# Leaving h undivided and subtracting the expert weights in PSUM at the start of an attention plus max-out kernel

## The chip, the cores and the metric

One core of one Trainium2 chip. The metric is the device time of one execution in microseconds (us), lower is better. The kernel before takes 340.46 us (median of 3 runs, 340.42 to 340.65). Executions vary by some tenths of a microsecond. A run counts as fast here if it lies within 1.5% of the fastest of its kernel.

## The reference

```python
# B, N, m, C = 4, 12544, 32, 128; d_ff = 1024
def mab(q, kv):
    s = scale * (q @ kv.transpose(0, 2, 1))
    a = softmax(s)                      # cut: max subtracted, exp, divided by the sum
    return a @ kv
h = mab(inducing, x)                    # 32 summary rows for each batch
y = mab(x, h)                           # every token attends to the 32 rows
h1, h2 = y @ w1, y @ w2
out = np.maximum(h1, h2) @ w_out
```

Everything after the second softmax is linear in `y` except the maximum. The kernel uses max(h1, h2) = h1 + relu(h2 - h1), so it needs w21 = w2 - w1 and, for each batch, two small products that stand in for the wide ones: hwd = h·w21 (32 rows by 1024) and m1 = h·(w1·w_out) (32 rows by 128).

## The kernel before

The batches run one after the other. While batch b makes outputs, batch b+1's h is computed in the gaps. Only batch 0 has nothing to hide behind: its first phase is about 16 us of transposes, scores and sums, in "units" of up to 16 tiles of x (128 tokens each), and the handover to the outputs follows. PSUM is the memory that matmuls write into; to "evict" is to copy a result out of one of its banks, on VectorE or ScalarE. The change touches these two stretches.

```python
units = []                              # 16 tiles each; the last full group in two 8s
for i, (_, n) in enumerate(p1_blocks):
    step = 8 if i == NP1 - 2 else n
    units += [(i, g, min(step, n - g)) for g in range(0, n, step)]
units = units[:-3] + units[-1:] + units[-3:-1]
...
def u_h():                              # batch 0: sums, reciprocal, h divided
    nc.vector.reduce_sum(out=rec, in_=<PSUM sums viewed as m x 4>)
    nc.vector.reciprocal(out=rec, in_=rec)
    nc.vector.tensor_mul(hT4, <h in PSUM, four copies>, <rec, four copies>)
...
u_h()
for i in range(4):                      # w21 = w2 - w1, fp32 in, fp16 out
    eng = nc.vector if i == 3 else nc.gpsimd
    eng.tensor_sub(w21[:, sl], w2f[:, sl], w1f[:, sl])
...
prep_w1T()                              # transposes of w1, copies on ScalarE
...
stages[-1][0].stage()                   # attention scores and exp of the first block
small_hwd(0)                            # hwd = h . w21: 4 matmuls, evicted by VectorE and ScalarE
for blk in stages[-1][1:]: blk.stage()
prep_w1out()                            # w1out = w1 . w_out
```

Then comes the steady loop. A "burst" multiplies exp values by hwd into four PSUM banks, and VectorE and ScalarE evict them through relu. A "final" makes one output bank: the m1 term (`m1d` is m1 spread over four masked copies by GpSimd), then 16 matmuls of relu by w_out. The first blocks use the `start` branch:

```python
def final(self, i):
    for s, (q, tt) in enumerate(cols):
        if start:
            nc.tensor.matmul(out=o, lhsT=<exp>, rhs=st[blk.b]["m1d"][:, q, :],
                             start=(s == 0), stop=False)
        for jb in range(NJB):
            nc.tensor.matmul(out=o, lhsT=self.relu[:, jb, q, tt, :], rhs=woutp[:, jb, :], ...)
    nc.vector.tensor_mul(self.osb[...], ps, rp)     # divide by the row sums, then store
```

The softmax here doesn't subtract the row's maximum and nothing guards it: scores larger than these inputs give would overflow.

## Time and profile before

| | before |
|---|---|
| median of 3 runs | 340.46 us |
| profiled run, span of the core | 340.25 us, 338.5 us |
| TensorE busy | 329.7 us, 97% |
| warm-up ends (start of the transpose of the inducing rows) | 7.32 us |
| VectorE starts on the sums | 23.62 us |
| first burst, third burst | 26.19, 29.11 us |
| last output multiplication starts | 335.35 us |

The times in the lower rows are starts in the timeline of the trace, counted from the start of the span. TensorE (PE) is busy nearly always, so what counts is where it is not: before 40 us. In the lines of a timeline the columns are start, duration, engine, source line, operation, out<-in, shapes and count; a bracket says how long the engine had been idle and what ended that.

### The profile page before, as it was taken

Reading aid. Unit: us, or ns where it says so; the run is one execution under the profiler, and the core shown is the slowest. Engines: PE = TensorE matmul, PEld = TensorE weight load, DVE = VectorE, ACT = ScalarE, POOL = GpSimd, SP = SyncE. Lnnn points to the kernel's source line nnn. Section 1 sums busy time; section 2 is a strip of 40 time slices with the busy share of each in tenths; the row PEclk is TensorE's granted clock in tenths of the full one; section 3 lists DMA queues with packets and bytes.
Section 4 is the critical chain, followed back from the end, with each engine's and each line's share of the span. In section 5 each row is a group of like instructions: output and inputs, shape, how many; then the busy total and the mean of one; then the engine's idle time right before and its main releaser. Section 6 shows DMA issues by size and latency. Waiting matters only on the chain.

```text
span 338.5 us, 14493 instructions
## 1 busy us (share of the span) xinstructions
PE 329.7 (97%) x6346; PEld 263.8 (78%) x6346; DVE 295.9 (87%) x620; ACT 269.7 (80%) x521; POOL 92.9 (27%) x164
## 2 busy tenths in 40 slices
PE   8899999999999999999999999999999999999996
PEld 3787688888768878888777878887777777878875
DVE  1348999999989999999998999999998998989994
ACT  1559988777888887787899777877899989888881
POOL 7243113454532224443242141423242100000000
PEclk9999999999999999999999999999999999999999
DMA  7999799499719985994229951212221221222222
GB/s 130 211 270 214 193 244 255 131 193 232 203 64 181 275 180 129 195 244 141 88 95 205 273 174 65 95 71 90 96 95 67 100 99 72 95 96 95 97 97 108
DMA packets 53423, 50.42 MB, mean 149 GB/s; under 512 B 41456, under 2 KB 42128, under 8 KB 53360
## 3 DMA queue, kind: packets, MB, share of 16 engines
q0 software_dynamic: 11408, 33.43, 37.0%
q1 hardware_dynamic: 41952, 16.08, 21.9%
q8 instruction: 49, 0.80, 1.0%
q14 instruction: 14, 0.11, 0.1%
HBM read 27.28 MB, written 25.69 MB: 157 GB/s over the span
## 4 chain that ended last, share of the span: by engine, by line
PE 93%; ACT 3%; DVE 1%; POOL 1%; issue 1%; DVEq 0%; POOLq 0%
PE ps L544 56%; PE ps L471 19%; PE ps L486 4%; PE ps L297 2%; PE ps L275 2%; PE ps L406 2%; PE ps L173 2%; PE ps L192 2%; ACT relu L508 1%; ACT xT L200 1%; PE ps L208 1%; PE ps L427 1%; PE ps L350 1%; DVE relu L504 1%; POOL eacc L324 1%
## 5 line engine op out<-in xcount | busy, mean ns | idle before, releaser
L508 ACT ACTIVATE relu<-ps 128x512 f16<-128x512 f32 x444 | 235.5, 601 | 43.0 <-PE ps L471 29.7
L504 DVE TENSOR_SCALAR relu<-ps 128x512 f16<-128x512 f32 x340 | 218.7, 679 | 5.3 <-PE ps L471 4.5
L544 PE MATMUL ps<-woutp,relu 128*128 128x128 f16 x3136 | 209.1, 220 | 0.0
L544 PEld LDWEIGHTS <-relu 128*128 128x128 f16 x3136 | 176.4, 98 | 29.8 <-issue 20.2
L560 DVE TENSOR_TENSOR o<-ps,rp 128x256 f32<-128x256 f32 x196 | 81.9, 418 | 16.0 <-PE ps L544 14.2
L570 POOL DMA_DIRECT2D out_dram<-o x75 | 41.1, 547 | 156.4 <-DVE o L560 108.1
L471 PE MATMUL ps<-e,hwd 32*128 32x256 f16 (+1 forms) x1632 | 82.8, 268 | 0.4
L471 PEld LDWEIGHTS <-hwd 32*128 32x128 f16 x1632 | 27.0, 92 | 19.0 <-issue 3.2
L486 PE MATMUL ps<-m,e 32*128 32x128 f16 x372 | 29.7, 214 | 0.7
L486 PEld LDWEIGHTS <-e 32*128 32x128 f16 x372 | 18.2, 92 | 7.0 <-issue 3.9
L317 POOL TENSOR_TENSOR eacc<-eacc,et 128x512 f32<-128x512 f32 (+1 forms) x18 | 18.5, 1028 | 0.3
L284 ACT ACTIVATE et<-ps 128x512 f16<-128x512 f32 (+1 forms) x21 | 11.4, 544 | 4.8 <-PE ps L275 4.8
L416 ACT ACTIVATE e<-ps 128x512 f16<-128x512 f32 (+2 forms) x30 | 14.9, 553 | 0.0
L114 POOL DMA_DIRECT2D xn<-in_x_dram x21 | 11.5, 550 | 4.7 <-DMA xn<-in_x_dram 4.1
L197 DVE COPY xT<-ps 128x1024 f16<-128x1024 f16 (+1 forms) x8 | 5.1, 642 | 8.4 <-PE ps L192 8.4
L200 ACT COPY xT<-ps 128x1024 f16<-128x1024 f16 x5 | 5.1, 1012 | 9.0 <-PE ps L192 9.0
L275 PE MATMUL ps<-inducingT,xT 128*128 128x32 f16 x294 | 10.6, 176 | 0.0
L297 PE MATMUL ps<-et,xn 128*128 128x32 f16 x294 | 10.6, 176 | 0.0
L275 PEld LDWEIGHTS <-xT 128*128 128x128 f16 x294 | 9.6, 96 | 0.0
L297 PEld LDWEIGHTS <-xn 128*128 128x128 f16 x294 | 9.5, 96 | 0.0
L173 PE MATMUL ps<-warm 128*128 128x512 f16 x22 | 7.7, 495 | 1.2 <-DVE warm L158 1.2
L406 PE MATMUL ps<-xT,hT 128*32 128x512 f16 (+2 forms) x120 | 8.7, 350 | 0.1
(65 smaller groups left out, 115.4 us busy)
## 6 DMA issues: line engine op xcount, KB each, us to landing
out_dram<-o POOLq DMA_DIRECT2D x72, 256.0 KB, 3.2
xn<-in_x_dram POOLq DMA_DIRECT2D x23, 512.0 KB, 8.9
out_dram<-o SPq DMA_DIRECT2D x24, 256.0 KB, 2.0
wf<-in_moe_w_dram POOLq DMA_DIRECT2D x2, 512.0 KB, 13.7
xn<-in_x_dram POOLq DMA_DIRECT2D x2, 256.0 KB, 13.5
out_dram<-o POOLq DMA_DIRECT2D x3, 128.0 KB, 4.7
xT<-xn SPq DMA_TRANSPOSE x21, 6.2
xn<-in_x_dram POOLq DMA_DIRECT2D x4, 64.0 KB, 9.3
```

Source lines behind the costliest of these rows:

```text
L275: nc.tensor.matmul(out=ps[:, j * M : (j + 1) * M], lhsT=xT_tiles[b % 2][:, k0 + j, :], rhs=inducingT, start=True, stop=True,)
L297: nc.tensor.matmul(out=ps[:, 0:M], lhsT=xn[:, j, :], rhs=et[:, j, :], start=(j == 0), stop=(j == n - 1),)
L317: nc.gpsimd.tensor_add(out=acc, in0=acc, in1=et[:, 0:n, :])
L406: nc.tensor.matmul(out=ps[32 * q : 32 * (q + 1), 0 : self.width], lhsT=st[self.b]["hT4"][:, 32 * q : 32 * (q + 1)], rhs=xT[:, q % self.g], ...
L416: nc.scalar.activation(out=self.e2[:, 0 : self.width], in_=ps[:, 0 : self.width], func=AF.Exp, scale=scale,)
L471: nc.tensor.matmul(out=ps[:, jj * w : (jj + 1) * w], lhsT=st[blk.b]["hwd"][r, 128 * jb : 128 * (jb + 1)], rhs=blk.e2[r, 128 * self.t0 : 12 ...
L486: nc.tensor.matmul(out=part.fin[q][1][:, 128 * s : 128 * (s + 1)], lhsT=part.blk.e2[r, 128 * tt : 128 * (tt + 1)], rhs=st[part.blk.b]["m1" ...
L504: nc.vector.tensor_scalar(out=dst, in0=src, scalar1=0.0, scalar2=None, op0=ALU.max)
L508: nc.scalar.activation(out=dst, in_=src, func=AF.Relu)
L544: nc.tensor.matmul(out=o, lhsT=self.relu[:, jb, q, tt, :], rhs=woutp[:, jb, :], start=False, stop=(s == 1 and jb == NJB - 1),)
L560: nc.vector.tensor_mul(self.osb[:, h : h + 2, :], ps[:, 0:256].rearrange("p (s c) -> p s c", s=2), rp.broadcast_to((128, 2, 128)),)
L570: eng.dma_start(out=outr[blk.b, :, k : k + nst, :], in_=self.osb[:, 0:nst, :])
```

## The change

Its intent is to shorten the serial path between the last sum of batch 0 and the first burst. There are five parts, and one piece of setup for the second.

1. The last full group of tiles comes as 8, 4 and 4, so that less work follows the last tile of x.
2. h is not divided by the softmax sums. It is scaled by 2^-14 to fit fp16, and the reciprocal sums become per-partition scales of the exp and of the evictions of hwd and m1.
3. w1 and w2 are loaded as fp16, and h·w2 - h·w1 is formed in PSUM by 8 matmuls in place of 4.
4. w1's transposes and w1out move behind hwd, and `m1d`'s matmuls move behind the 16 relu matmuls.
5. Later batches still need w21. An fp32 reload of both weights by SyncE (SP) and four subtractions on GpSimd move into the loop.

The sums over one column need a mask, `same_m`. VectorE builds it with four copies at the start of the first phase.

```diff
+        if i == NP1 - 2:
+            units += [(i, 0, n // 2), (i, n // 2, n // 4), (i, n // 2 + n // 4, n // 4)]
...
-        nc.gpsimd.dma_start(out=w1f, in_=moe_w1)
-        nc.gpsimd.dma_start(out=w2f, in_=moe_w2)
+        nc.gpsimd.dma_start(out=w2h, in_=moe_w2)
+        nc.gpsimd.dma_start(out=w1h, in_=moe_w1)
...                                         (after the inducing rows are transposed)
+        for q in range(4):
+            r = slice(32 * q, 32 * (q + 1))
+            nc.vector.tensor_copy(
+                out=same_m[r, :, :], in_=identity32[r, None, r].broadcast_to((32, 4, M))
+            )
...                                         (u_accum: sums over a column of ones)
-                    lhsT=ones16,
-                    rhs=et[:, j : j + w // M, :],
+                    lhsT=et[:, j : j + w // M, :],
+                    rhs=ones16,
...                                         (u_h)
+            part = smp.tile([128, 2], F32, name="sum_part")
+            nc.vector.tensor_mul(part, <sums>, sum_scale)
+            nc.tensor.matmul(out=ps[:, 0:2], lhsT=same_m, rhs=part, start=True, stop=True)
+            nc.vector.tensor_scalar(out=hT4, in0=<h in PSUM>, scalar1=HS, op0=ALU.mult)
+            nc.vector.reciprocal(out=rs, in_=ps[:, 0:2])
+            nc.scalar.mul(neg, hT4, -1.0)
...                                         (u_hwd, new)
+            for lhsT, rhs, first_mm in ((hT4, w2h, True), (neg, w1h, False)):
+                for i, (bi, ps) in enumerate(banks):
+                    nc.tensor.matmul(out=ps[:, 0:w], lhsT=lhsT, rhs=rhs[...],
+                                     start=first_mm, stop=not first_mm)
+            ... evictions scaled by st[0]["rs"] on VectorE and ScalarE
...                                         (Block.stage)
-                    scale=scale,
+                    scale=st[self.b]["scale"],
...                                         (final: the m1d matmuls after the relu matmuls)
...                                         (order)
-        small_hwd(0)
+        u_hwd()
         for blk in stages[-1][1:]:
             blk.stage()
-        prep_w1out()
+        prep_w1T()
...
+        def load_wf():
+            nc.sync.dma_start(out=w1f, in_=moe_w1)
+            nc.sync.dma_start(out=w2f, in_=moe_w2)
+        at(24, load_wf)
+        for i in range(4):
+            at(33 + 2 * i, sub_w, i)
...
-            p.burst(u, lead, (lambda: small_m1(0)) if g == 0 else None)
+            p.burst(u, lead, (prep_w1out, lambda: small_m1(0))[g] if g < 2 else None)
```

## The prediction

> **What bounds the kernel now.** I read the busy row of the page, the stages, the chain of work that ended last, the timeline of the first 36 us, and the waits on DMA. The page and its chain of work:
>
> ```profile
> PE 329.7 (97%) x6346; PEld 263.8 (78%) x6346; DVE 295.9 (87%) x620; ACT 269.7 (80%) x521; POOL 92.9 (27%) x164
> ...
> PE ps L544 56%; PE ps L471 19%; PE ps L486 4%; PE ps L297 2%; PE ps L275 2%; PE ps L406 2%; PE ps L173 2%; PE ps L192 2%; ACT relu L508 1%; ACT xT L200 1%; PE ps L208 1%; PE ps L427 1%; PE ps L350 1%; DVE relu L504 1%; POOL eacc L324 1%
> ```
>
> TensorE is on the chain for 93% of the span, three quarters of it in L544 and L471, the expert's output and input matmuls, which the change leaves alone. The stages (columns: window, sum of its width, PE, PEld, DVE, ACT, POOL busy us) say where there is room:
>
> ```profile
> 10.00:20.00 10.00, 9.13 (x210) 8.35 (x211) 2.77 (x4) 6.15 (x8) 2.50 (x4) 1.00 1.08 238
> 20.00:30.00 10.00, 9.44 (x202) 7.48 (x199) 7.02 (x17) 6.96 (x19) 5.40 (x10) 1.00 1.18 234
> 30.00:40.00 10.00, 9.60 (x159) 6.84 (x154) 9.36 (x19) 9.61 (x20) 1.46 (x3) 1.00 0.95 208
> ...
> 100.00:200.00 100.00, 99.90 (x1991) 81.25 (x1988) 93.28 (x196) 83.60 (x163) 32.12 (x57) 1.00 0.79 182
> ```
>
> From 40 us on PE has nearly no gap, so the change can only move the start of that stretch. Before it lie batch 0's first phase (to 23.6 us) and its handover into the first small blocks; from 30 to 36 us VectorE and ScalarE are full of evictions. The handover, from the timeline (start, duration, engine, line):
>
> ```profile
> 22.36 0.86 ACT L217 ACTIVATE et<-ps 128x64 f16<-128x64 f32 x3 [0.91 <-PE ps L208]
> ...
> 23.62 0.29 DVE L253 TENSOR_REDUCE hrec<-ps 128x32 f32<-128x128 f32 x1 [1.62 <-PE ps L233]
> ...
> 23.94 0.35 DVE L258 RECIPROCAL hrec<-hrec 128x32 f32<-128x32 f32 x1
> 24.29 1.07 ACT L617 CAST w1T<-ps 128x512 f16<-128x512 f32 x2 [1.07 <-PE ps L611]
> 24.41 0.29 DVE L260 TENSOR_TENSOR hT<-ps,hrec 128x128 f16<-128x128 f32 x1
> ...
> 25.25 0.76 DVE L355 CAST hwd<-ps 128x256 f16<-128x256 f32 x2 [0.22 <-PE ps L350]
> ...
> 26.19 0.40 PE L471 MATMUL ps<-e,hwd 32*128 32x128 f16 x16
> ...
> 26.86 0.27 ACT L375 CAST m<-ps 128x128 f16<-128x128 f32 x1 [0.30 <-PE ps L370]
> ...
> 27.02 1.09 ACT L508 ACTIVATE relu<-ps 128x512 f16<-128x512 f32 x2
> ...
> 27.21 1.18 POOL L378 TENSOR_TENSOR m1d<-m,mask 128x256 f16<-128x256 f16 x2 [0.37 <-ACT m L375]
> ...
> 29.11 1.09 PE L471 MATMUL ps<-e,hwd 32*128 32x128 f16 x24
> ```
>
> The reader is to see a serial path: last sum matmul, then 1.08 us on VectorE (23.62 to 24.70), 1.49 us to the first burst (26.19), then 2.92 us until the third burst starts at 29.11. I take 29.11 as the anchor: ScalarE is busy without a break from 29.54 to 38.8, so a shift of the third burst passes into the rest.
>
> **What the Trainium skill says.** "TensorE: Matmul & The Clock Gate", section Back-to-back issue gap, gives about 25 ns for up to 64 columns, 134 cycles for 128 and 262 for 256 at 2.4 GHz. The trace agrees: 16 accumulations of 32 columns take 0.39 us in the chain (24 ns each), 16 transposes of 128 columns 0.91 (57 ns), and I use 0.11 us for one of 256. "VectorE: DVE Perf Modes", section The perf-mode tier table, lets a copy from PSUM run at up to 2x; the copy of 1024 fp16 columns out of PSUM took 0.69 us, below the 1.07 that 1024 columns take at one per 0.96 GHz clock, so it agrees. "DMA: Bandwidth & Descriptors", section SWDGE vs HWDGE vs iDMA, ties a cast during DMA to GpSimd: the fp16 weights stay behind x in the POOL queue, whereas the later fp32 reload may go by SP. No run yet shows either kind for the weights. "ScalarE: Activation LUTs", section Step-by-step: what each stage is for, lets the scale be a per-partition pointer at no extra stage; no row of before shows one, so I charge it nothing.
>
> **The change part by part.**
> *Shorter last units.* Units of x become 16 x5, 2, 8, 4, 4 tiles. The order of instructions shows that the fifth unit's transposes now come before the fourth's scores. Landings before (time of issue plus time to landing, read for each load): fourth unit 14.05 us, fifth 17.2, the 2 tiles 17.5, the two 8s 18.75 and 20.1. So the last tiles still land at 20.1. Worked forward with the durations of before: transposes of unit four 15.60 to 16.5, accumulation to 17.0, wait for the fifth unit, its transposes 17.4 to 18.3, scores of four to 18.7, the 8 tiles' transposes to 19.3, scores of five to 19.7, accumulation to 20.2. VectorE, which takes all of the last copies at 0.69 per 1024 and about 0.42 (estimate between 0.29 and 0.69) per 512 columns, ends them at about 21.4. The last scores run 21.7 to 21.8, their exp (128 columns, 0.27) ends at 22.2, the last sum matmul lands at 22.5. Before, VectorE started on the sums at 23.62: gain 1.1 us. The order also has one warming matmul fewer; it lies inside that.
> *Sums over one column.* 25 matmuls of mostly 128 columns become 25 of one column: 25 x (57 - 25) ns = 0.8 us of PE, but nearly all beside the ScalarE copy (19.28 to 20.29 for instance) that paces each 2.58 us unit. Worth 0.05 in the last units, counted above.
> *h undivided.* Removed: 0.29 + 0.35 + 0.29. Added on VectorE: a 2-column product (0.16, like the 0.17 reciprocal of 4 columns) and h's eviction (0.29), so h is ready 22.97, 0.47 after the start in place of 1.08. The fp32 sum matmul (0.25, as L331's) and a 2-column reciprocal end at 23.16, beside PE's work. Gain 0.6.
> *Subtraction in PSUM.* Four matmuls of 256 columns more: 4 x 0.11 = 0.44 later. The negation on ScalarE (0.27, from 23.0) hides beside the first four. The evictions (2 x 0.38 on each engine) end at 24.75, first burst about 24.83 in place of 26.19: gain 1.36 at this point, which is near 1.1 + 0.6 - 0.44 = 1.26, the rest being issue gaps.
> *w1's transposes.* In fp16: 8 x 0.057 in place of 8 x 0.13 of PE, but moved behind the hwd matmuls (24.2 to 24.66). Their copy goes to VectorE after its two hwd evictions: 24.85 to 25.54, so w1out's matmuls run 25.6 to 26.05, against 25.64 to 26.26 before. Here the gain stops.
> *Order on ScalarE.* After: w1out (26.25 to 26.52), two relus (1.10, to 27.62), e of the 8-tile block (0.41, to 28.03), then m (0.27, to 28.30). Before, m came in front of the relus and was done at 27.13. GpSimd's m1d (0.60 for the half the first output needs) therefore ends at 28.98, against 27.80.
> *m1d matmuls last.* The first output's 16 matmuls may start at 27.7 instead of 28.2 and end 28.6, then wait for m1d until 29.05. Third burst: 29.17, against 29.11.
> *Weights.* x fills the queue in both, and one DMA slot more shifts no landing that is waited for: the fp16 pair is estimated at 21.3 and 22.6, where fp32 landed, woutp at about 24.2. The w21 subtractions (4 x 0.72 on GpSimd) move to the bursts around 80 to 92 us, before its fold at 91.6. GpSimd idles 1.0 to 2.4 us before each output there and one fits into each, so I charge nothing. The order of the main loop is otherwise unchanged, engine for engine.
> Sum: -1.1 - 0.6 + 0.44 before the first burst, and about +1.3 given back by w1T, w1out, m and m1d: +0.06 at the anchor, with an error of some 0.6 as each of a dozen waits can be off by 0.05 to 0.1 and some by more.
>
> **The rivals.** (a) The gain of the first burst survives: evictions of bursts 0 and 1 start up to 1 us earlier on VectorE (25.6 against 26.62), the m1d wait is shorter than I think, and the rest of the ramp follows. Speaks for it that 30 to 36 us are bound by evictions. It gives at most 340.46 - 1.3 = 339.2. (b) The worked path: m1d takes the place of the old wait; 340.5. (c) GpSimd's later subtractions delay the fold that PE waits 0.97 us for at 93.66, or the reload of w1 and w2 slows x or the transposes. Against it: one subtraction is 0.72 and the gaps are longer, and DMA is at about half. If all four landed in the path it would be 2.9 us: 343.4. (d) DMA stays the floor of the first phase and the smaller loads are slower; then the 1.1 shrinks to 0.5 and, with the unchanged path behind it, the time is 341.1.
>
> **Range and chances.** I weigh (b) at 0.45, (a) in part or whole at 0.4, (c) and (d) at 0.15. The mean of (b) 340.5 and a half-surviving gain, 339.7, is about 340.1; I predict 340.1 us, range 339.2 to 340.9. Two per cent is 6.8 us, more than the whole handover holds (23.6 to 29.1 us), so faster by over 2% has 0.01, slower 0.01, within 2% 0.98.
>
> **What would show it.** Right: sums reach VectorE at about 22.5; first burst at 24.7 to 25.0; w1out no earlier than 25.5; m1d's matmuls preceded by a PE gap of about 0.45 us near 28.6 to 29.05; third burst within 0.3 us of 29.1; the same 0.97 us wait near 93.7. Wrong: a third burst before 28.5 (then rival a), a PE gap at the fold over 1.5 us (rival c), or a last landing of x after 20.6 us (rival d). A change at the end of the kernel would also refute it, as nothing there has moved.

## The result and the profile after

The changed kernel took 341.17 us (median of 6 runs, 340.81 to 341.45), against 340.44 us (340.00 to 340.65) for the kernel before in the same rounds. The ratio is 1.0023, with a 95% interval of 1.0010 to 1.0036. A ratio here is the mean time of one kernel's fast runs over that of the other's of the same rounds, so not quite the ratio of the medians quoted. The class predicted, within 2%, came true, but the time lies 0.27 us above the top of the range, and 1.07 us above the predicted time. The kernel got slower by 0.7 us where I had expected it to gain 0.4.

The page of after, busy row and chain of work that ended last:

```profile
PE 328.4 (97%) x6351; PEld 263.1 (78%) x6351; DVE 297.3 (88%) x628; ACT 269.3 (79%) x520; POOL 94.6 (28%) x166
...
PE 87%; DMA 6%; issue 2%; POOL 1%; ACT 1%; DVE 1%; POOLq 0%
```

TensorE has 1.3 us less work, in a span 0.6 us longer. The 6% of DMA in the chain are less than they seem: at `m1d` the chain steps back through GpSimd's own queue to a weight load, with 4.25 us of "issue" between. The timeline below names what GpSimd really waited for, ScalarE's m. The stages of after, columns as in the prediction:

```profile
10.00:20.00 10.00, 8.94 (x223) 8.13 (x220) 4.02 (x7) 5.50 (x8) 3.03 (x5) 1.00 1.10 208
20.00:30.00 10.00, 8.66 (x194) 6.83 (x191) 6.15 (x17) 6.44 (x18) 3.31 (x6) 1.00 1.19 210
30.00:40.00 10.00, 9.41 (x155) 6.67 (x155) 9.34 (x20) 9.69 (x20) 1.15 (x2) 1.00 0.95 206
...
100.00:200.00 100.00, 99.91 (x1991) 81.07 (x1987) 93.53 (x196) 83.75 (x163) 32.62 (x57) 1.00 0.83 177
```

From 20 to 30 us PE is busy 8.66 us where it was 9.44: the handover holds more idle time, not less. The steady stage is as it was. The handover itself, from the timeline of after:

```profile
17.31 1.07 PE L202 MATMUL ps<-identity,xn 128*128 128x128 f16 x16 [0.26 <-DMA xn<-in_x_dram]
...
20.66 0.75 DVE L207 COPY xT<-ps 128x512 f16<-128x512 f16 x2 [0.43 <-PE ps L218]
...
22.70 0.16 DVE L264 TENSOR_TENSOR sum_part<-ps,sum_scale 128x2 f32<-128x2 f32 x1 [1.28 <-PE ps L243]
...
25.10 0.40 PE L534 MATMUL ps<-e,hwd 32*128 32x128 f16 x16
...
25.20 0.69 DVE L682 COPY w1T<-ps 128x1024 f16<-128x1024 f16 x1 [0.17 <-PE ps L678]
...
25.95 0.62 PE L688 MATMUL ps<-woutp,w1T 128*128 128x128 f16 x8 [0.45 <-DVE w1T L682]
...
26.61 0.27 ACT L696 CAST w1out<-ps 128x128 f16<-128x128 f32 x1 [1.25 <-PE ps L688]
...
26.77 1.09 ACT L571 ACTIVATE relu<-ps 128x512 f16<-128x512 f32 x2
...
27.74 0.49 ACT L479 ACTIVATE e<-ps,rs 128x256 f16<-128x256 f32 x1
...
28.10 0.39 ACT L436 ACTIVATE m<-ps,rs 128x128 f16<-128x128 f32 x1
...
28.57 1.19 POOL L441 TENSOR_TENSOR m1d<-m,mask 128x256 f16<-128x256 f16 x2 [4.29 <-ACT m L436]
...
29.23 0.27 PE L607 MATMUL ps<-m1d,e 128*128 128x128 f16 x2 [0.38 <-POOL m1d L441]
...
29.44 1.04 PE L534 MATMUL ps<-e,hwd 32*128 32x128 f16 x24
```

The sums are reached 0.92 us sooner and the first burst 1.09 us sooner (25.10 against 26.19). Then w1's transposed copy, w1out, two relus, m and m1d come one after another, and the third burst starts 0.33 us later than before. That is the path that the prediction worked out. The first line, the fifth unit's transposes waiting for DMA, is in the prediction too (17.4); the wait is new against the kernel before, and its end differs from run to run.

The end of each timeline, first before, then after:

```profile
335.35 0.42 DVE L560 TENSOR_TENSOR o<-ps,rp 128x256 f32<-128x256 f32 x1 [0.58 <-PE ps L544]
```

```profile
335.56 0.42 DVE L624 TENSOR_TENSOR o<-ps,rp 128x256 f32<-128x256 f32 x1 [0.58 <-PE ps L607]
```

The last output is 0.21 us later, but the span is 0.6 us longer (338.5 to 339.1). So 0.39 us arise after the last computation.

I cut every trace at the same five points: W, the end of the warm-up; S, VectorE's first instruction on the sums; the third burst; the last output multiplication; the end of the span.

| stretch, us | before | after | difference |
|---|---|---|---|
| start to W | 7.32 | 6.98 | -0.34 |
| W to S (first phase) | 16.30 | 15.72 | -0.58 |
| S to third burst (handover) | 5.49 | 6.74 | +1.25 |
| third burst to last output | 306.24 | 306.12 | -0.12 |
| last output to the end | 3.15 | 3.54 | +0.39 |
| sum (span) | 338.5 | 339.1 | +0.6 |

The spans are read to 0.1 us, so each tail, here and below, may be off by 0.05.

The first row is chance, not the change (the mean W of all fifteen traces is 7.32 us, as in this trace of before). The granted clock goes from half to full at some time between 4.2 and 7.2 us after the start of the span, differently in each run (in the trace of before at 5.5 us), and W lies between 6.66 and 8.14 us in the traces. That alone can scatter the times by some ±0.7 us. There is a second scatter. In 10 of the 44 runs of the kernel before in the jobs of the experiments, the mean granted clock is 0.995 where it is otherwise 0.998 or more; nine of these ten take 341.8 to 342.3 us and one 342.9, some 1.5 us longer than the rest. None of the 12 runs of the changed kernel did this, too few to say that the change prevents it. I give the median of the before runs at 0.998 or more ("full clock"), which is 340.46, 340.60, 340.62 and 340.57 us in the four jobs.

### The profile page after: what moved, and what is told of

It is laid out like the page before. It is cut to its first block, busy times and chain, and to the rows that moved or that the text cites. A ratio compares the mean times of both kernels' runs of the same rounds, so it can differ in the third digit from the quotient of the medians.

```text
span 339.1 us, 14513 instructions
## 1 busy us (share of the span) xinstructions
PE 328.4 (97%) x6351; PEld 263.1 (78%) x6351; DVE 297.3 (88%) x628; ACT 269.3 (79%) x520; POOL 94.6 (28%) x166
## 4 chain that ended last, share of the span: by engine, by line
PE 87%; DMA 6%; issue 2%; POOL 1%; ACT 1%; DVE 1%; POOLq 0%
PE ps L598 56%; PE ps L534 19%; PE ps L549 4%; DMA w1h<-in_moe_w_dram 3%; DMA xn<-in_x_dram 3%; PE ps L322 2%; PE ps L300 2%; PE ps L469 2%; ACT relu L571 1%; PE ps L490 1%; DVE relu L567 1%; POOL eacc L349 1%; DVE o L624 1%; PE ps L410 0%; PE ps L607 0%
## 5 line engine op out<-in xcount | busy, mean ns | idle before, releaser
L207 DVE COPY xT<-ps 128x1024 f16<-128x1024 f16 (+2 forms) x10 | 5.7, 595 | 6.8 <-PE ps L202 6.2
L479 ACT ACTIVATE e<-ps 128x512 f16<-128x512 f32 (+1 forms) x21 | 10.9, 577 | 0.0
L210 ACT COPY xT<-ps 128x1024 f16<-128x1024 f16 x4 | 4.0, 1012 | 8.1 <-PE ps L202 8.1
L183 PE MATMUL ps<-warm 128*128 128x512 f16 x21 | 7.0, 482 | 1.2 <-DVE warm L166 1.2
```

## The experiments

My theory after reading the traces: the handover goes as worked out; the loss over it comes from the end (an order of closing waits that two more DMAs shift), from a first phase that a landing holds, and from pointer scales that I charged nothing. The rivals: noise in the warm-up; the reload of the weights slowing the loop; the order in `final`. Thirteen kernels ran, in four jobs. The stretches inside a trace repeat well: the changed kernel run again gave the same 6.74 us from S to the third burst.

| run | median us | before at full clock, same job | W to S | S to third burst | S to 7th output | tail |
|---|---|---|---|---|---|---|
| before | 340.44 | | 16.30 | 5.49 | 18.11 | 3.15 |
| after | 341.17 | | 15.72 | 6.74 | 19.36 | 3.54 |
| a0, after again | 341.18 | 340.46 | 15.94 | 6.74 | 19.36 | 3.50 |
| x1, constant scales | 341.47 | 340.46 | 15.78 | 6.57 | 19.19 | 3.52 |
| x2, m1d first | 343.22 | 340.46 | 15.48 | 8.22 | 21.12 | 3.47 |
| x3, w1T early | 340.72 | 340.46 | 15.20 | 6.75 | 19.37 | 3.54 |
| t1, reload in eight | 340.89 | 340.60 | 15.18 | 7.16 | 19.78 | 3.11 |
| t2, before with two more DMAs | 340.94 | 340.60 | 16.30 | 5.49 | 18.11 | 3.44 |
| t4, units of before | 341.34 | 340.60 | 16.24 | 6.77 | 19.39 | 3.52 |
| y2, w1out before the burst | 340.00 | 340.60 | 15.13 | 6.67 | 19.29 | 3.14 |
| u1, units alone | 340.41 | 340.62 | 15.93 | 6.00 | 18.62 | 3.12 |
| x3c, w1T early, banks apart | 340.79 | 340.62 | 15.49 | 6.47 | 19.06 | 3.52 |
| y3, y2 with banks apart | 340.92 | 340.62 | 15.75 | 5.91 | 18.65 | 3.09 |
| z1, no reload | 340.63 | 340.57 | 15.60 | 6.75 | 19.37 | 3.15 |
| y4, all together | 340.49 | 340.57 | 15.48 | 5.50 | 18.12 | 3.12 |

"7th output" is the start of the seventh output multiplication, some 12 us past the third burst and beyond the crowded first blocks; "tail" runs from the start of the last output multiplication to the end of the span. Each stretch is from the one profiled run.

### a0: the changed kernel again

> The changed kernel unaltered, to have its times in the same rounds as the experiments beside it. Both theories: about 341.2 us (ratio 1.0023 to the kernel before). The trace of the first look had the third burst at 29.44 us against 29.11; if this trace again has it 0.2 to 0.4 us later than before's, the loss in the handover is not chance. If the third burst lies level with before's and the time is still up, the loss is elsewhere (rival: the reload of the weights and the later subtractions, or the end of the kernel).

No edit. Median 341.18 us (340.65 to 341.58), 0.72 above the before runs at full clock, as the first 0.73. The ratio of all fast runs is 1.0004 (0.9977 to 1.0031), because three of the eleven before runs of this job have the 0.995 clock. Handover and tail repeat within 0.04 us; W to S does not (15.94 against 15.72).

### x1: constants in place of the pointer scales

```diff
-                        scalar1=st[0]["rs"],
+                        scalar1=0.75,
-                    nc.scalar.mul(hwd[:, sl], ps[:, 0:w], st[0]["rs"])
+                    nc.scalar.mul(hwd[:, sl], ps[:, 0:w], 0.75)
-                nc.scalar.mul(m1, ps[:, 0:128], st[0]["rs"])
+                nc.scalar.mul(m1, ps[:, 0:128], 0.75)
-                    scale=st[self.b]["scale"],
+                    scale=scale,
```

> The changed kernel with constants in place of the per-partition 1/sum in batch 0's exp, hwd and m evictions (result wrong by a factor near one, on purpose; all instructions stay, in number and order). Theory: reading the scale through a pointer costs 0.06 to 0.12 us an instruction, and two hwd evictions (0.12), e of the 8-tile block (0.08) and m (0.12) lie in the chain to m1d: third burst 0.3 us earlier, at 29.1, time about 340.9. Rival, that the pointer costs nothing on the path (as I predicted) and the loss comes after 40 us: third burst at 29.4 and 341.2.

The outputs are wrong by design (relative error 0.22). The groups by shape (count, then busy us and mean ns of one), a0 first, then x1:

```profile
L436 ACT ACTIVATE m<-ps,rs 128x128 f16<-128x128 f32 x1 | 0.4, 390 | 0.0
...
L479 ACT ACTIVATE e<-ps,rs 128x512 f16<-128x512 f32 x5 | 3.2, 697 | 0.0
```

```profile
L436 ACT ACTIVATE m<-ps 128x128 f16<-128x128 f32 x1 | 0.3, 309 | 0.0
...
L479 ACT ACTIVATE e<-ps 128x512 f16<-128x512 f32 x23 | 12.8, 621 | 0.0
```

A pointer scale adds 76 ns to an exp of 512 columns and 81 ns to m, whose plain copy before took 265 ns. An hwd eviction fell from 470 to 380 ns on ScalarE and from 480 to 420 on VectorE. So the cost that I left out is real. On the path it is worth 0.17 us (6.74 to 6.57), about half of the 0.3 that I expected of it: the first burst stays at S + 2.40 us with either scale, because it then stands behind w1's transposes on PE and not behind the evictions. The time, 341.47 us, shows none of it; the scatter is larger.

### x2: m1d's matmuls put back in front

```diff
+                    if start:
+                        nc.tensor.matmul(out=o, lhsT=<exp>, rhs=st[blk.b]["m1d"][:, q, :],
+                                         start=(s == 0), stop=False)
                     for jb in range(NJB):
                         ...
-                if start:
-                    (the same matmuls after the loop)
```

> The changed kernel with the m1d matmuls put back in front of the 16 relu matmuls in outputs that open their own bank. Theory: m1d is what PE waits for (29.23), so the 16 matmuls (0.90) move behind that wait: third burst at about 30.3, time 342.1. Rival, that the order inside the output is beside the path: 341.2.

Median 343.22 us, ratio 1.0061 (1.0033 to 1.0089). The timeline of x2:

```profile
29.61 0.22 PE L598 MATMUL ps<-m1d,e 128*128 128x128 f16 x1 [1.27 <-POOL m1d L441]
```

m1d arrives 6.54 us after S as in the changed kernel (6.53), but now 16 relu matmuls stand behind it, 16 x 57 ns = 0.9 us. That step of the change is right and necessary: without it, the new place of m costs 1.76 us up to the seventh output. About half of this, by estimate (1.76 less the 0.9), is another thing that I had not expected. The stages of x2 (the number after the POOL count is the granted clock):

```profile
31.00:32.00 1.00, 1.00 (x27) 0.78 (x26) 0.55 (x3) 0.07 (x1) 0.00 (x0) 0.50 1.07 217
```

From 30.0 to 33.4 us the clock is at half. Five of the six runs of x2 have a mean clock of 0.995 or less. The window follows a stretch in which PE was busy 0.73, 0.34 and, until 29.6 us, 0 of each microsecond; over the 3.41 us before the drop it was busy for 1.87.

### x3: w1's transposes in front of the sums' end

```diff
-        nc.gpsimd.dma_start(out=w2h, in_=moe_w2)
         nc.gpsimd.dma_start(out=w1h, in_=moe_w1)
+        nc.gpsimd.dma_start(out=w2h, in_=moe_w2)
...
+        w1t = prep_w1T()            # transposes only
         u_h()
+        prep_w1T_copy(*w1t)         # the copy, on VectorE, ahead of the hwd evictions
...
-        prep_w1T()
```

> The changed kernel with w1 loaded ahead of w2, w1's transposes before the sums' evictions and their copy on VectorE before the hwd evictions (VectorE idles there from 23.51 to 24.16). Theory: w1out's matmuls wait for the w1T copy, which ends at 25.9; freed of it they follow the first burst at 25.5, ScalarE's w1out copy starts at 26.15 in place of 26.61, and everything to m1d comes 0.4 to 0.5 earlier: third burst at 29.0, time 340.75. Rival, that the first burst or the later stretch binds and not w1T: third burst 29.4, time 341.2; or that w2, now landing second at 23.2, delays the hwd matmuls: above 341.2.

The handover stayed at 6.75 us: no gain. But the run does not test the idea: the first scores were given the PSUM bank of the sums and waited 0.37 us for the reciprocal to free it. The profiled run was also the slowest of the six (342.72 us). Median 340.72 us (340.59 to 342.72), ratio 1.0008. Inconclusive; x3c repeats it with the banks apart.

### t1: the reload as eight DMAs

```diff
-            nc.sync.dma_start(out=w1f, in_=moe_w1)
-            nc.sync.dma_start(out=w2f, in_=moe_w2)
+            for i in range(4):
+                sl = slice(256 * i, 256 * (i + 1))
+                nc.sync.dma_start(out=w1f[:, sl], in_=moe_w1[:, sl])
+                nc.sync.dma_start(out=w2f[:, sl], in_=moe_w2[:, sl])
```

> The changed kernel with the fp32 reload of w1 and w2 issued as eight transfers of 256 columns in place of two of 1024, same bytes. Theory for the end: SP's closing waits run over the DMA semaphores in a fixed order at 0.06 us each, and two more transfers on SP turned the last output's semaphore from the eighth place of that order to the second, so that six more waits come after its landing. Eight more transfers turn it full circle: from the last output's multiplication to the end 3.15 us as before, not 3.5, and the time 0.37 lower, about 340.8. The first sums to the seventh output multiplication stays 19.36 us. Rival, that the longer end comes from the landing itself: 3.5 us and 341.2.

A DMA reports its landing on a semaphore, a counter that an engine can wait for. The point of eight is that the DMA semaphores in use on SP come round to where they were. The raw semaphore records of the two first traces show what happens at the end (times in us; "wait" is when SP's closing wait on that semaphore is over):

```
before: last store lands 337.467 (semaphore 117)
  wait 108 336.248 ... wait 116 336.787, wait 117 337.484, wait 118 337.545, end of program 337.61
after:  last store lands 337.709 (semaphore 108)
  wait 108 337.726, 112 337.787, 113 337.852, 114 337.913, 115 337.972, 116 338.034,
  117 338.093, 118 338.155, end of program 338.22
```

SP waits for all DMA semaphores in a fixed order, 0.06 us each. Before, the last store's semaphore stood nearly last in that order, so that the other waits were over when it landed. The two extra loads by SP shift which semaphore the last store gets, to one of the first places, and seven waits follow its landing. With eight loads the tail is 3.11 us in place of 3.54. The median is 340.89 us, 0.29 above before at full clock in place of 0.72; ratio 0.9988 (0.9964 to 1.0012), five of eleven before runs being at 0.995. In this one trace the handover took 0.42 us more, the matmuls on w1h having started 0.4 us late; no other run shows this, and I have no cause for it.

### t2: the kernel before with two more DMAs by SP

```diff
+        for i in range(2):
+            spare = consts.tile([M, C], F32, name=f"spare{i}")
+            nc.sync.dma_start(spare, inducing)
```

> The kernel before with two more small loads on SP at its start (the inducing points again, into tiles that nothing reads). Theory for the end: the turn by two semaphores alone costs 0.37: last multiplication to the end 3.5 us in place of 3.15, time about 340.8 against 340.44, all else as before (first sums to seventh output multiplication 18.11). Rival: no change, 340.45.

The converse: nothing else is touched, handover and first phase are those of before to 0.01 us, and the tail goes from 3.15 to 3.44 us. Median 340.94 us, 0.34 above before at full clock (ratio 0.9993, 0.9971 to 1.0014, for the same reason as in t1). t1 and t2 together settle the end: it is the number of DMAs, and no work that the change does.

### t4: the changed kernel with the units of before

```diff
-        if i == NP1 - 2:
-            units += [(i, 0, n // 2), (i, n // 2, n // 4), (i, n // 2 + n // 4, n // 4)]
+        step = 8 if i == NP1 - 2 else n
+        units += [(i, g, min(step, n - g)) for g in range(0, n, step)]
         (and the order of the first phase as before)
```

> The changed kernel with the x units and the first phase's order of the kernel before. Theory: the new units bring the sums 0.4 to 1.1 us forward, as the traces say, depending on when the fifth unit lands, and the handover behind them is as long as in the changed kernel: warm-up's end to the sums 16.1 to 16.3, sums to seventh output multiplication 19.3 to 19.4, time 341.7 to 342. Rival, that the handover waits for something of fixed time (a landing), so that the earlier sums bought nothing: 341.2 and a handover shorter by what the sums are later.

W to S is 16.24 us, as in before (16.30), and the handover 6.77, as in after. Without the shorter units the first phase thus loses all but 0.06 us of what it gained; with them it is 15.72 and 15.94 us in the two traces of after. But the 0.06 is the difference of two larger effects that neither the prediction nor the plan of t4 names. The mask copies keep VectorE busy at the start, and the first scores wait for its copy of x. First two lines of after, then one of before:

```profile
8.02 0.91 DVE L671 COPY same_m<-identity 32x128 f32<-32x128 f32 x4
...
9.70 0.56 PE L218 MATMUL ps<-inducingT,xT 128*128 128x32 f16 x16 [1.14 <-DVE xT L207]
```

```profile
9.23 0.37 PE L208 MATMUL ps<-inducingT,xT 128*128 128x32 f16 x8 [0.34 <-DVE xT L197]
```

The second unit's transposes begin at W + 3.35 us in t4 and in after, at W + 3.11 in before, so by these traces the mask costs 0.24 us. From the fifth unit's transposes to S, t4 takes 5.12 us and before 5.43. The one-column sums are the edit that touches this stretch, so they appear to be worth about 0.3 us there, not the 0.05 of the prediction. In after the 0.24 is hidden, because the fifth unit's landing is waited for in any case. Median 341.34 us (ratio 1.0003), 0.74 above before at full clock; that is below the 341.7 to 342 expected, although both stretches came out as expected.

### y2: w1out in front of the first burst

x3, and:

```diff
         u_hwd()
+        prep_w1out()
...
-            p.burst(u, lead, (prep_w1out, lambda: small_m1(0))[g] if g < 2 else None)
+            p.burst(u, lead, (lambda: small_m1(0)) if g == 0 else None)
         (reload in eight; the bank of the sums counted busy 2 us longer)
```

> The changed kernel with w1 loaded first, its transposes before the sums' evictions, their copy on VectorE in the gap before the hwd evictions, w1out before the first burst, m ahead of the first relus, and the reload in eight transfers. Theory: the chain w1T, w1out, relus, e, m, m1d is what gave the gain back, so with it out of the path the sums-to-seventh-multiplication stretch falls from 19.36 to 18.2 to 18.5 and the end to 3.15: about 339.7 to 340.0, under the kernel before. Rival, that evictions of the first blocks bind and not this chain: the stretch stays above 19 and the time above 340.5.

```profile
25.10 0.24 PE L469 MATMUL ps<-xT,hT 128*32 128x128 f16 x4 [1.13 <-DVE w1T L686]
```

In the timeline the second scores wait 1.13 us for the bank of the w1 transposes: another collision of banks, made by my edit. The handover gains only 0.07 us. The median of 340.00 us (339.32 to 341.74) is the lowest of all, ratio 0.9967 (0.9941 to 0.9993), 0.60 below before at full clock. Its runs spread over 2.4 us, the profiled one was the slowest of them (341.74 us), and the stretches of its trace do not explain the figure, so I don't build on it.

### u1: the shorter units in the kernel before

```diff
-        step = 8 if i == NP1 - 2 else n
-        units += [(i, g, min(step, n - g)) for g in range(0, n, step)]
+        if i == NP1 - 2:
+            units += [(i, 0, n // 2), (i, n // 2, n // 4), (i, n // 2 + n // 4, n // 4)]
         (and the order of the first phase as in the changed kernel; the rest is before)
```

> The kernel before with nothing but the shorter last units and their order. Theory: the sums come 0.4 to 1.1 us earlier, but the first use of w21 waits for GpSimd's three subtractions, which end 2.1 us after the fp32 weights land at 22.5, thus at 24.7, so at least half of it is lost before the first burst: sums to first burst grows from 2.57 to 2.9 or more, time 340.0 to 340.4. Rival, that the units' gain comes through whole: 339.5 or less.

Median 340.41 us (ratio 0.9993, 0.9966 to 1.0020), or 340.39 without its one run at 0.995: 0.2 below before. W to S falls by 0.37 us, and the handover grows by 0.51. The timeline says why:

```profile
22.93 2.28 POOL L667 TENSOR_TENSOR w<-wf 128x256 f16<-128x256 f32 x3 [3.15 <-DMA wf<-in_moe_w_dram]
...
25.27 0.38 PE L353 MATMUL ps<-w,hT 128*128 128x256 f16 x2 [0.35 <-POOL w L667]
```

The fp32 weights land at about 22.8 us, and the subtractions on GpSimd take 2.28 us from there. With the sums early, hwd waits for them. So the subtraction in PSUM is not an ornament of the change: it appears to be what lets an earlier sum become an earlier burst (S + 2.40 us in after, S + 3.08 here, S + 2.57 in before, where the subtractions are ready in time). No run isolates it from the undivided h.

### x3c: x3 with the banks apart

```diff
-            model.bank_free[bi] = model.ev("DVE", 2, end, 0.1)
+            model.bank_free[bi] = model.ev("DVE", 2, end, 0.1) + 2.0
-            model.bank_free[bi] = model.ev("DVE", 512, end)
+            model.bank_free[bi] = model.ev("DVE", 512, end) + 5.0
```

> The changed kernel with only w1's part moved forward (loaded first, transposes before the sums' evictions, copy before the hwd evictions), again with the banks kept apart, w1out still behind the first burst, m behind the relus. Theory: the wait of w1out's matmuls for the w1T copy (0.45 us in the changed kernel) is gone and the stretch to the seventh multiplication falls by about that, from 19.36 to 18.9; end 3.5. Rival: no fall, 19.3 or more.

These lines only steer which PSUM bank the kernel's own planner hands out next. Now the early transposes are worth 0.27 us up to the third burst and 0.30 to the seventh output (19.06), two thirds of the 0.45 that I expected: m still comes behind the relus. Median 340.79 us (ratio 1.0011, 0.9978 to 1.0045), 0.17 above before at full clock with the bad tail still in it.

### y3: y2 with the banks apart

y2, and:

```diff
-            model.bank_free[bi] = model.ev("DVE", 512, end)
+            model.bank_free[bi] = model.ev("DVE", 512, end) + 5.0
```

> The version with w1out before the first burst again, with the first score stage of the second phase kept out of the PSUM bank of the w1T copy, for which it had waited 1.13 us. Theory: the sums-to-first-burst stretch is 2.5 to 2.7 us and sums to seventh output multiplication 18.2 to 18.5 (19.36 in the changed kernel, 18.11 before); with the sums at 22.7 to 23.1 and the end at 3.15 the time is 339.5 to 340.0, below the kernel before. Rival, that the first blocks' evictions bind: stretch above 19, time above 340.5.

The third burst comes at S + 5.91 us, 0.83 sooner than in after, and m1d no longer holds PE. Yet the median is 340.92 us, ratio 1.0001 (0.9970 to 1.0032). The trace loses it later:

```profile
77.36 0.46 PE L322 MATMUL ps<-et,xn 128*128 128x32 f16 x12 [0.46 <-issue]
```

PE stands for 0.46 us at 77 us, and the loop from seventh to last output takes 294.28 us in place of 293.50. x3, x3c and y2 show such stops between 70 and 91 us as well (loops of 294.97, 293.95 and 294.3), while a0, x1 and t4, with the same reload, do not. The traces of x3 and y2 are each from the slowest run of its kernel, those of x3c and y3 are not.

### z1: no reload, w21 from the fp16 weights

```diff
-            nc.gpsimd.tensor_sub(w21[:, sl], w2f[:, sl], w1f[:, sl])
+            nc.gpsimd.tensor_sub(w21[:, sl], w2h[:, sl], w1h[:, sl])
-        at(24, load_wf)
```

> The changed kernel with w21 of the later batches taken from the fp16 weights that are in the core already, so no reload at all; the four subtractions stay where they are. Theory (the reload costs only the turn of the semaphores): end 3.15 in place of 3.5, first sums to seventh output 19.36, seventh output to last output 293.5 as before; time about 340.8. Rival (the reload also slows the loop through the busy DMA): the stretch from the seventh to the last output falls below 293.4 and the time below 340.6.

The result stays correct. Tail 3.15 us, handover 6.75, loop 293.55. Median 340.63 us in a tight 340.47 to 340.85, ratio 0.9999 (0.9986 to 1.0011). Taking away the reload takes away the loss of the tail, and nothing that the loop's length shows (293.50 us in after). The seven loads of x for batch 2 take 5.0 to 9.4 us to land, against 6.0 to 9.6 in before and 6.3 to 11.2 in after; but a0, with the reload, has 5.9 to 9.3, so the reload is not shown to slow them. Against before at full clock the median is 0.06 us higher, where after was 0.7: more than the tail's 0.39, and the traces don't say where the rest went.

### y4: all together

y3 without the reload, with the fp16 subtraction of z1, and m1 called right after the first burst's relus, ahead of the next scores and exp:

```diff
-            p.burst(u, lead, (lambda: small_m1(0)) if g == 0 else None)
+            p.burst(u, lead)
+            if g == 0:
+                small_m1(0)
         (bank offsets 1.0 and 1.5 us)
```

> w1 first, w1T and w1out before the first burst, m after the first block's relus and ahead of e, no reload, banks kept apart. Theory: m1d is no longer waited for and the relus are not held up by m, so first sums to seventh output falls to 18.0 to 18.4 (18.65 with m ahead of the relus, 19.36 in the changed kernel), the loop is 293.5 without the extra stop that y3 showed, the end 3.15; with the sums at 22.9 the time is 339.5 to 339.9, under the kernel before. Rival (the first blocks' evictions bind): 18.6 or more and 340.2 or more; or a stop in the loop again without a reload, 293.8 or more.

```profile
22.46 0.16 DVE L264 TENSOR_TENSOR sum_part<-ps,sum_scale 128x2 f32<-128x2 f32 x1 [1.29 <-PE ps L243]
...
26.37 0.37 ACT L436 ACTIVATE m<-ps,rs 128x128 f16<-128x128 f32 x1
...
27.75 0.28 PE L607 MATMUL ps<-m1d,e 128*128 128x128 f16 x2
...
27.96 1.12 PE L534 MATMUL ps<-e,hwd 32*128 32x128 f16 x24
```

m now starts 3.91 us after S in place of 5.40, m1d's matmuls have no idle time in front, and the third burst comes 1.15 us earlier than in before (27.96 against 29.11), with a handover as short as before's. The profiled run took 339.57 us. The median is 340.49 us (339.31 to 340.97), ratio 0.9989 (0.9971 to 1.0007): 0.7 us below the changed kernel's median, though in another job, and against before not clear of the noise. Three of its six runs lie at 340.8 to 341.0. Even the profiled one has a loop of 294.1 us, half a microsecond over that of z1, with PE waiting 0.3 us for a transposed tile of x. So the stops in the loop come without the reload too. What makes them stays open.

## Why the prediction failed

**The handover: right, though the hundredths are luck.** The steps for the divided h (0.6) and the PSUM subtraction (+0.44) give a first burst at 24.83 - 22.5 = 2.33 us after the sums; measured 2.40. In the trace h is ready at S + 0.40 us (1.08 before) and the first burst follows 2.00 us later (1.49 before); no run takes the two steps apart. What ends the wait for the first burst was w1's transposes on PE and not the evictions (x1 leaves it at 2.40; x3c, without the transposes there, has 2.21). The serial path of w1T, w1out, relus, m and m1d gives a third burst at 29.17 - 22.5 = 6.67 us; measured 6.74, twice. The idle time ahead of m1d's matmuls was to be about 0.45 us and was 0.38. m ended 5.80 us after the sums in the working and 5.79 in the trace. The idea that the third burst gives the gain back stood. That m fits to 0.01 us is errors that cancel: w1out came 0.16 us late against the sums and e and m were each about 0.1 longer than worked, while consecutive instructions on ScalarE overlap by 0.11 to 0.13 us in the trace (the relus end at 27.86, e starts at 27.74), which the working had set end to end.

**"gain 1.1 us" of the shorter units: too large.** This is the first mis-sized term. In before, the first phase ran from W without a stop (16.30 us in its trace and again in t2's, with W 0.28 us later), so its sums move with the luck of the warm-up. With the shorter units the fifth unit is wanted earlier, and in eight of the twelve traces PE waits for its landing: 0.26 us in after, 0.63 in a0, 0.33 in x1, 0.51 in u1. Its transposes started between 17.06 and 17.91 us in these four, where the working had 17.4, and the sums came 5.2 to 5.5 us behind them, not 5.1. In after the last copy of x ends at 21.41 us, as worked, but the last scores, exp and sum matmul take 1.29 us more in place of 1.1. Over all twelve the shortfall of 0.4 is about half a later start of the fifth unit (17.62 us on average, not 17.4) and half the work behind it (5.29, not 5.1). So an early warm-up helps little where the landing is late. Over the twelve traces with shorter units the sums begin at 22.91 us on average, 0.71 before the 23.62 of before, whose W is the mean one. Rival (d) named DMA as the floor, with a gain of 0.5, and shared a small part of 0.15 with (c). Its other half, slower small loads, did not come: the last tiles of x landed at 20.16 us in after, not after 20.6. What moves the fifth unit's landing (16.3 to 17.9 us) no run tested, and no run took the mask copies away.

**"A change at the end of the kernel would also refute it, as nothing there has moved": it was there.** The tail measured +0.39 us, and t1, t2 and z1 show that the two loads by SP caused it through the order of the closing waits. This is the step that is simply missing from the sum. I had looked at the reload only for what it does to bandwidth.

**"so I charge it nothing": wrong, but small.** A pointer scale costs 76 to 90 ns on ScalarE; on the path to the third burst it measured 0.17 us. The handover came out right in spite of it, because of the overlaps named above.

**The weighing.** The worked path gave 340.5. I moved the prediction to 340.1 because rival (a), a surviving gain, got 0.4. The path had been worked instruction by instruction and nothing in the profile spoke against it: (a) rested on waits that I might have got wrong, and the traces of after and a0 show that I had not. The move is 0.4 of the 1.07 us, the tail another 0.39, and the smaller gain of the first phase 0.39 (1.1 - 0.71); they come to 1.18, the loop gives 0.12 back, and the handover's own 0.07 is left out. Of the signs that it set, the third burst missed too: 29.44 us in after and 29.88 in a0, where it allowed 29.1 ± 0.3.

**Rival (c), the weights.** PE waited 1.00 us before the fold's matmul near 94 us, against 0.97 before, and z1, without the reload, has the same loop (293.55 us against 293.50). Charging it nothing there was right.

**The sum.** With the mean gain of the first phase, -0.71 + 1.25 - 0.12 + 0.39 = +0.81 us, against 0.73 and 0.72 us between the medians of the two comparisons. The runs within one kernel scatter by as much as that, so I take it as agreement and no finer test. The handover's 1.25, the 0.71 of the first phase and the tail's 0.39 are each shown by several traces; so is the loop's 0.12 (306.07 to 306.17 us in after, a0, x1, t1, t4 and z1, 306.17 to 306.26 in before, t2 and u1; 0.11 apart on average).

## What to carry to other kernels

When a step on a serial path is shortened, work out what comes next on it to the point where all engines are full: here the first burst gained 1.09 us and the third lost 0.33, because a small product had been put behind two evictions (y4, which moved w1's transposes, w1out and m ahead, gave it back). Count added DMAs by the queue and the semaphores they take, not only by bytes: two loads in the middle of the kernel made its end 0.3 to 0.4 us longer. And when a path has been worked through instruction by instruction, don't average it with a hope; spend the doubt on the ends that the sum leaves out.

## What the Trainium skill lacked or had wrong

- "ScalarE: Activation LUTs": the section Step-by-step: what each stage is for, which the prediction rests on, calls the affine step free. The page does have a cost, in its later section What ACT_TABLE_LOAD costs: about 93 ns for each per-partition pointer operand. The runs agree roughly: 76 ns on an exp of 512 columns (697 against 621), 81 on one of 128 (372 against 291), 90 on an hwd eviction (470 against 380). The figure would serve better beside the word "free".
- No page has the closing waits: about 0.06 us for each DMA semaphore, in a fixed order, so that the place of the last store's semaphore is worth up to 0.4 us (tails of 3.09 to 3.15 against 3.44 to 3.54 us).
- "TensorE: Matmul & The Clock Gate", section What's actually happening, ties the return to half clock to one idle window of about 3.4 us. In x2 a half-clock window of 3.4 us (30.0 to 33.4) came after a wholly idle stretch of only 1.27 us, with PE busy 0.73 and 0.34 in the two microseconds up to 29.0, and 1.87 of the 3.41 us before the drop. The length of the window fits the page; an idle window does not need full idleness in this trace. A later section of the page, A second HAM failure mode: psum-queue depth-cycling, does tell of a clock that drops from many short idle times, but gives no busy share; no run here tells where the limit lies.
